# Sparse attention and a gated layer on one core: zero products into the open PSUM sums in the planner's idle stretches

## The chip, the cores and the metric

The kernel runs on one core of one Trainium2 chip. The metric is the device time of one execution in microseconds (us), the median of several runs of the same program; less is better. Engines are named as the profile names them: PE is the matrix engine (PEld its weight loads), DVE the vector engine, ACT the scalar engine, POOL the general engine, SP the engine from whose queue all DMA transfers of this kernel are issued.

## The reference

Two steps follow each other: a block-sparse attention over 4 batches of 8 heads, 768 positions and 64 columns, and a layer of 512 to 2048 to 512 columns with a rational function between its two products.

```python
scores = scale * np.matmul(q, k.transpose(0, 1, 3, 2))
mask = near blocks | first and last block | 3 sampled blocks per block of 32 rows
attn = exp(scores - max); attn = attn / (sum + 1e-09)      # masked
x = np.matmul(attn, v), heads side by side                 # 3072 x 512
h = x @ w_in
P = a[0] + a[1] * h + a[2] * h**2 + a[3] * h**3
Q = 1.0 + abs(b[0]) * abs(h) + abs(b[1]) * h**2
out = (P / (Q + 1e-06)) @ w_out                            # 3072 x 512
```

## The kernel before

The work is written down first as a list of operations (`Op`), each with an engine or a choice of engines, a price in ns, the operations that it comes after, a priority and the buffers it takes. Nothing is issued while this list is made. At the end `issue` runs through a time line of its own: at each step it takes, over all engines, the operation that can start first by its prices, writes that instruction down as the next one of its engine, and moves the engine's time forward. The order on each engine, and for the operations with a choice also the engine, come out of that time line alone. On the chip each engine then runs its row in that order, and waits by semaphores only.

The attention goes block by block (96 blocks of 32 query rows): scores (line 903, into the PSUM tile `sp`), masked maxima on DVE (913), exponentials on ACT (931), transposition (972, `pt`), its copy out of PSUM (`pT`, by `times`, line 150 on ACT), product with the values (1029, `av`). Four blocks make a half of a chunk of 256 rows, which is weighed (1063, `xn`) and transposed (1075). The layer goes in 96 units, 8 for each of 12 chunks (`unit(c, u)`): `into` (1140 to 1142, PSUM tile `ph`), the rational function on ACT and DVE (1147 to 1185, ending in `gh` and `gl`), and `out_of` (1196 to 1198), which adds the unit's products into the chunk's PSUM tile `acc`. A chunk's sum stays open from its first unit to its last. Chunk 0 is split: its first four units come first, then the eight of chunk 1, then its other four; between them a part of its sum waits in SBUF.

In the first quarter of the run the weights are also decoded from 64-bit words: loads `wl` (430, 433), three DVE steps on integers (442, 445, 448), a copy `wo_h` (`times`; ACT at line 150 or POOL at line 154), the remainder `wo_l` on POOL (459), and the like for `wi`. The keys and queries are scaled and split (`hl`, `hlq`) with the same choice of engine.

`fill` (line 157) writes a product that nobody reads. It uses the identity `ident16` as both operands and a tile `acc` of its own out of the pool of which the real sums take theirs, and starts and ends a sum with it (line 162). In `issue` the branch for PE writes such products wherever its own time line has PE waiting, as long as that time is below `fend`, 80,000 ns. Below `fend` too, it puts up to two of them ahead of an operation when its account of the current window is less than `fsh` full. That account (`tick`, `work_of`) also says whether the planner takes PE's clock to be warm; when it does not, PE's prices are multiplied by 1.8 or 2. The times of the planner's line are not those of the chip.

Of the kernel before, what the change touches and what calls it, by code (L numbers as in the profile page):

```python
# [13 lines left out]
F16 = mybir.dt.float16  # L14
# [9 lines left out]
def kernel(  # L24
# [27 lines left out]
    nc = tc.nc  # L52
    B, H, S, D = q.shape
    DM, DFF = out.shape[1], w_out.shape[0]
    P = 128
    BLK = 32
# [17 lines left out]
    const = ctx.enter_context(tc.tile_pool(name="const", bufs=1))  # L74
# [17 lines left out]
    ident16 = const.tile([P, P], F16, name="ident16")  # L92
# [60 lines left out]
        else:  # L153
            eng.tensor_scalar(out=out, in0=in_, scalar1=by, scalar2=0.0, op0=ALU.mult, op1=ALU.add)

    fills = []

    def fill():

        if not fills:  # L160
            fills.append(ps_acc.tile([P, CH // P, DM], F32, name="acc"))
        nc.tensor.matmul(fills[0][:, 0].rearrange("p (n m) -> p n m", n=DM // P), ident16, ident16.rearrange("p (o m) -> p o m", o=1).broadcast_to([P, DM // P, P]), start=True, stop=True)

    def issue(ahead):
# [11 lines left out]
        now = dict.fromkeys(todo, 500.0)  # L176
# [13 lines left out]
        fsh = 0.8  # L190
        other = {VE: 500, SC: 534.0, PO: 243.0}
        unit_of = {VE: nc.vector, SC: nc.scalar, PO: nc.gpsimd}
        slack, fend, f00, fgap = 21.0, 80000, 3000, 0
        while left:
            best = None
            for e, l in todo.items():
# [15 lines left out]
            e = o.eng  # L212
# [6 lines left out]
            if isinstance(price, list):  # L219
                for ns, size in price:  # L220
                    t = max(t, lanes.pop(0) if e == SY else t) + ns
                    dma = max(dma, t + 650) + size / 225.0
                    if e == SY:
                        lanes.append(dma + 900)
                end = dma + 900
            elif e == TE:
                f0 = max(now[e], f00)
                while f0 < fend:
                    tick(f0)
                    f = 213 if warm else 427  # L230
                    if f0 + f + fgap > t:
                        break
                    fill()
                    work_of(f0, f, 1.0)
                    f0 += f
                tick(t)
                if now[e] < fend:
                    w = window
                    x0 = w * 3413
                    for _ in range(2):  # L240
                        if not warm or t - x0 < 700 or busy.get(w, 0.0) >= fsh * (t - x0):
                            break
                        fill()
                        work_of(t, 213, 1.0)
                        t += 213
                if not warm:
                    price *= 2 if price > 1100 or price < 500 else 1.8
                work_of(t, price, o.work)
                end = t = t + price
            else:  # L250
                end = t = t + price
# [871 lines left out]
    def unit(c, u):  # L1123
# [63 lines left out]
        def out_of(e):  # L1187
            def run():
                if new and e == 0:
                    accs[c] = ps_acc.tile([P, CH // P, DM], F32, name="acc")  # L1190
                acc = accs[c]
                f = 2 * u + e
                for t in range(CH // P):
                    ghs = d["gh"][:, e * CH + t * P:e * CH + (t + 1) * P]
                    gls = d["gl"][:, e * CH + t * P:e * CH + (t + 1) * P]
                    nc.tensor.matmul(acc[:, t], ghs, wo_h[:, f], start=(new and e == 0), stop=False)  # L1196
                    nc.tensor.matmul(acc[:, t], ghs, wo_l[:, f], start=False, stop=False)  # L1197
                    nc.tensor.matmul(acc[:, t], gls, wo_h[:, f], start=False, stop=(last and e == 1))  # L1198
            return run

        def piece(lows, tiles):
# [164 lines left out]
```

## Time and profile before

| | us |
|---|---|
| median of 3 runs | 883.18 |
| lowest and highest run | 882.15, 884.92 |
| profiled execution, its own time | 884.27 |
| its span, first to last instruction | 882.5 |
| PE busy | 828.6 |
| DVE busy | 733.3 |
| ACT busy | 676.5 |
| POOL busy | 110.9 |

The last five lines belong to the one profiled execution. What lies between its time and its span is ahead of the first and behind the last instruction. An engine's busy time is the part of the span in which it ran an instruction; the time in which it stood is the rest. The granted clock is a share of full speed: 1.00 is 2.4 GHz and 0.50 is 1.2 GHz; a stretch with a value between had both. The tables by stretch are the views that show which engine is full at which time, and the chain of waits says which instruction set the time of the next.

### The profile page before, as it was taken

How to read it: one execution, taken by the hardware profiler on the slowest of the kernel's cores; microseconds unless marked ns; L12 is line 12 of the kernel's file. 1: busy time of each engine (PE TensorE's matmuls, PEld its weight loads, DVE VectorE, ACT ScalarE, POOL GpSimd, SP SyncE). 2: the span in 40 equal slices, each digit the busy share in tenths (PEclk: the TensorE clock that was granted, in tenths of full speed). 3: DMA queues.
4: the chain of work that ended last, by engine and by line, in shares of the span. 5: the costliest groups of instructions: out<-in, count | busy, mean ns of one | idle time of the engine just before them, and what ended most of it. 6: DMA issues, size and time to landing. Idle time of an engine off the chain costs nothing.

```text
span 882.5 us, 27171 instructions
## 1 busy us (share of the span) xinstructions
PE 828.6 (94%) x10339; PEld 645.5 (73%) x10339; DVE 733.3 (83%) x1749; ACT 676.5 (77%) x1447; POOL 110.9 (13%) x117
## 2 busy tenths in 40 slices
PE   8979686797899999989999999999999999999997
PEld 3545465675678787778888887777788888888886
DVE  5658998999999888778887888887878887788886
ACT  6787897897687988788867888888767688767563
POOL 1113631616310000100000000100000000000000
PEclk9999897798999999999999999999999999999999
DMA  7798689878856966799556967889556766730000
GB/s 200 178 187 197 173 181 201 221 194 228 176 150 165 287 161 159 181 214 254 168 142 160 257 179 198 199 225 259 149 144 176 200 170 156 180 106 26 1 26 24
DMA packets 240209, 151.16 MB, mean 171 GB/s; under 512 B 16208, under 2 KB 222928, under 8 KB 240080
## 3 DMA queue, kind: packets, MB, share of 16 engines
q1 hardware_dynamic: 240080, 149.43, 68.4%
q8 instruction: 82, 1.34, 0.7%
q14 instruction: 47, 0.39, 0.2%
HBM read 132.07 MB, written 11.01 MB: 162 GB/s over the span
## 4 chain that ended last, share of the span: by engine, by line
PE 70%; DVE 10%; DMA 7%; ACT 6%; SPq 4%; issue 2%; POOL 1%; ACTq 0%; DVEq 0%; POOLq 0%
PE acc L1196 9%; PE ph L1140 9%; PE acc L1198 9%; PE acc L1197 9%; PE ph L1141 8%; PE ph L1142 8%; PE av L1029 5%; PE sp L903 5%; PE pt L972 5%; DMA vg<-in_v_dram 2%; DMA wl<-in_moe_w_in_dram 2%; DMA wl<-in_moe_w_out_dram 1%; ACT kt L150 1%; PE sp L753 1%; ACT pr L931 1%
## 5 line engine op out<-in xcount | busy, mean ns | idle before, releaser
L1140 PE MATMUL ph<-xh,wi 128*128 128x256 f16 x768 | 213.5, 278 | 0.0
L1141 PE MATMUL ph<-xl,wi 128*128 128x256 f16 x768 | 212.2, 276 | 0.0
L1142 PE MATMUL ph<-xh,wi 128*128 128x256 f16 x768 | 211.9, 276 | 0.0
L1196 PE MATMUL acc<-wo_h,gh 128*128 128x512 f32 x376 | 160.4, 427 | 0.2 <-ACT ld L150 0.2
L1198 PE MATMUL acc<-wo_h,gl 128*128 128x512 f32 x376 | 150.0, 399 | 2.1 <-DVE gl L1185 2.1
L1197 PE MATMUL acc<-wo_l,gh 128*128 128x512 f32 x376 | 149.3, 397 | 0.8 <-POOL wo_l L459 0.8
L1164 DVE SCALAR_TENSOR_TENSOR ab<-sq,absb,ab 128x512 f32<-128x512 f32 x96 | 74.4, 775 | 49.9 <-ACT ab L1161 49.7
L1147 ACT ACTIVATE sq<-ph,fc 128x512 f32<-128x512 f32 x96 | 65.6, 684 | 56.9 <-PE ph L1142 56.3
L1140 PEld LDWEIGHTS <-wi 128*128 128x128 f16 x768 | 76.0, 99 | 29.2 <-issue 16.2
L913 DVE CUSTOM_DVE_ANT_1 pr<-sp,bias 128x256 f32<-128x256 f32 x224 | 84.9, 418 | 8.8 <-PE sp L903 8.4
L931 ACT ACTIVATE pr<-pr,st,cqb 128x256 f32<-128x256 f32 x112 | 66.1, 594 | 32.9 <-DVE st L942 32.9
L1175 DVE SCALAR_TENSOR_TENSOR gh<-tt,par,rr 128x512 fp32r<-128x512 f32 x96 | 72.4, 754 | 21.4 <-PE acc L1197 20.3
L1198 PEld LDWEIGHTS acc<-wo_h,gl 128*128 128x128 f32 x376 | 71.2, 189 | 19.9 <-DVE gl L1185 3.0
L1196 PEld LDWEIGHTS acc<-wo_h,gh 128*128 128x128 f32 x376 | 71.5, 190 | 17.3 <-issue 2.5
L1029 PE MATMUL av<-vg,pT 128*32 128x64 f32 x3584 | 75.6, 227 | 9.0 <-DMA vg<-in_v_dram 5.6
L1142 PEld LDWEIGHTS <-wi 128*128 128x128 f16 x768 | 76.2, 99 | 9.7
L1029 PEld LDWEIGHTS av<-vg,pT 128*32 128x32 f32 x3584 | 57.9, 113 | 33.8 <-issue 12.0
L1141 PEld LDWEIGHTS <-wi 128*128 128x128 f16 x768 | 76.2, 99 | 8.0
L972 PE MATMUL pt<-ident,pr 128*128 128x128 f32 x448 | 74.9, 289 | 7.5 <-ACT pT L150 6.8
L972 PEld LDWEIGHTS pt<-ident,pr 128*128 128x128 f32 x448 | 68.3, 205 | 18.0 <-ACT pT L150 8.0
L1197 PEld LDWEIGHTS acc<-wo_l,gh 128*128 128x128 f32 x376 | 71.4, 190 | 13.1 <-POOL wo_l L459 1.7
L150 ACT ACTIVATE pT<-pt 128x512 f32<-128x512 f32 x112 | 66.2, 591 | 14.8 <-PE pt L972 14.2
(165 smaller groups left out, 1671.6 us busy)
## 6 DMA issues: line engine op xcount, KB each, us to landing
vg<-in_v_dram SPq DMA_DIRECT2D x312, 64.0 KB, 3.4
vg<-in_v_dram SPq DMA_DIRECT2D x88, 192.0 KB, 4.0
vg<-in_v_dram SPq DMA_DIRECT2D x24, 512.0 KB, 5.7
kall<-ks SPq DMA_DIRECT2D x49, 192.0 KB, 3.6
kall<-ks SPq DMA_DIRECT2D x147, 64.0 KB, 2.0
ld<-in_k_dram SPq DMA_DIRECT2D x36, 256.0 KB, 5.0
wl<-in_moe_w_in_dram SPq DMA_DIRECT2D x32, 256.0 KB, 5.0
wl<-in_moe_w_out_dram SPq DMA_DIRECT2D x16, 512.0 KB, 4.5
```

The source lines that it names most:

```text
L150: nc.scalar.activation(out=out, in_=in_, func=AF.Copy, scale=by)
L913: nc.vector.tensor_tensor_reduce(out=prs[x][:, g].rearrange("p (s r) -> p s r", r=BLK), in0=h["sp"][:, g].rearrange("p (s r) -> p s r", r= ...
L931: nc.scalar.activation(out=prs[x][:, g], in_=prs[x][:, g], func=AF.Exp, scale=Q["first"]["c"], bias=st[:, 6 + g:7 + g], accum_out=total if ...
L972: nc.tensor.transpose(pp[:, jj * P:(jj + 1) * P], cols, ident)
L1029: nc.tensor.matmul(av[rows, g], pT[:, 2 * g + kt, rows] if plain else pT[:, 2 * g + kt, pa_, rows], vf[:, g * HG + h4, kt * D:(kt + 1) * D ...
L1140: nc.tensor.matmul(o, wh, xh[:, :, cc], start=(cc == 0), stop=False)
L1141: nc.tensor.matmul(o, wh, xl[:, :, cc], start=False, stop=False)
L1142: nc.tensor.matmul(o, wl, xh[:, :, cc], start=False, stop=(cc == NCC - 1))
L1164: nc.vector.scalar_tensor_tensor(out=d["ab"], in0=d["sq"], scalar=absb[:, 1:2], in1=d["ab"], op0=ALU.mult, op1=ALU.add)
L1196: nc.tensor.matmul(acc[:, t], ghs, wo_h[:, f], start=(new and e == 0), stop=False)
L1197: nc.tensor.matmul(acc[:, t], ghs, wo_l[:, f], start=False, stop=False)
L1198: nc.tensor.matmul(acc[:, t], gls, wo_h[:, f], start=False, stop=(last and e == 1))
```

## The change

There is a tile of zeros, `zeros16`, written once by DVE at the start. When a real sum is open, `fill` now adds a product of the identity and that tile to the sum's first half, `acc[:, 0]`, without starting or ending a sum: it adds zeros. When no real tile `acc` has been taken yet, it does as before. `summing` holds the open sums; `out_of` enters a chunk with its first product and takes it out with its last. The planner's limit `fend` goes from 80,000 to 280,000 ns, and between two sums nothing is filled in.

```diff
+    zeros16 = const.tile([P, BLK], F16, name="zeros16")
+    nc.vector.memset(zeros16, 0.0)
+    fills, summing = [], {}
...
+        if summing:
+            acc = next(iter(summing.values()))
+            nc.tensor.matmul(acc[:, 0].rearrange("p (n m) -> p n m", n=DM // BLK), ident16, zeros16.rearrange("p (o m) -> p o m", o=1).broadcast_to([P, DM // BLK, BLK]), start=False, stop=False)
+            return
...
-        slack, fend, f00, fgap = 21.0, 80000, 3000, 0
+        slack, fend, f00, fgap = 21.0, 280000, 3000, 0
...
-                while f0 < fend:
+                while f0 < fend and (summing or not accs):
...
-                if now[e] < fend:
+                if now[e] < fend and (summing or not accs):
...
+                if e == 0:
+                    summing[c] = acc
...
+                if last and e == 1:
+                    del summing[c]
```

On PE the changed program has 219 of the old products where there were 201, and 111 of the new ones. Up to its 1,422nd row PE's order is the same as before; from there the order of the real work differs too, on all engines, since the planner's time line is another. Both orders meet at the same amount of real PE work (16 units into `ph`, 13 out, 880 score products), row 3490 before and row 3749 now.

The first place is on PE, behind the second unit's products into `acc`. Before, the scores of the next block (`sp`, 903) come right behind them. Now ten zero products stand between (one is shown), and the value product and the transposition have moved ahead. Line numbers of the changed kernel are 7 to 9 higher.

```order
L972 MATMUL pt_2426<-ident_91,pr_2296 128x128 x4
L1196 MATMUL acc_2345<-wo_h_105,gh_1958 128x512
L1197 MATMUL acc_2345<-wo_l_106,gh_1958 128x512
L1198 MATMUL acc_2345<-wo_h_105,gl_2168 128x512
...
L903 LDWEIGHTS qa_2082
L903 MATMUL sp_2467<-kall_108,qa_2082 32x96
```

```order
L1205 MATMUL acc_2300<-wo_h_107,gh_2051 128x512
L1206 MATMUL acc_2300<-wo_l_108,gh_2051 128x512
L1207 MATMUL acc_2300<-wo_h_107,gl_2296 128x512
L1036 MATMUL av_115<-vg0_111,pT_2417 32x64 x16
L979 MATMUL pt_2477<-ident_91,pr_2291 128x128 x4
L165 LDWEIGHTS ident16_96
L165 MATMUL acc_2300<-zeros16_98,ident16_96 128x512
...
L910 LDWEIGHTS qa_2292
L910 MATMUL sp_2527<-kall_110,qa_2292 32x96
```

What moved: PE runs ten products more before it reaches the scores.

The second place is the last block of zero products, behind the transposition of the eighth group of queries (`hlq`). Before, the transposed probabilities and the next products into `ph` follow at once. Now 16 zero products come first, then products into `acc`, a transposition and four more zero products.

```order
L753 LDWEIGHTS hlq_4335
L753 MATMUL sp_4410<-ident16_96,hlq_4335 128x128
...
L972 MATMUL pt_4423<-ident_91,pr_4217 128x128 x4
L1140 LDWEIGHTS wi_104
L1140 MATMUL ph_4431<-xh0_114,wi_104 128x256
```

```order
L760 MATMUL sp_4539<-ident16_96,hlq_4493 128x128
...
L165 MATMUL acc_3630<-zeros16_98,ident16_96 128x512
...
L1205 MATMUL acc_3630<-wo_h_107,gh_4534 128x512
L1206 MATMUL acc_3630<-wo_l_108,gh_4534 128x512
L1207 MATMUL acc_3630<-wo_h_107,gl_4576 128x512
...
L979 MATMUL pt_4610<-ident_91,pr_4135 128x128 x4
...
L910 LDWEIGHTS qa_4561
L910 MATMUL sp_4625<-kall_110,qa_4561 32x256
```

What moved: the products into `ph` that followed the transposition are now behind twenty zero products and the next block's scores.

The third place is POOL, where the weights' remainders `wo_l` are made, at its fifth such step. Before, POOL also made the copy `wo_h` ahead of the second remainder. Now that copy is ACT's, and one of four that left POOL.

```order
L459 TENSOR_TENSOR wo_l_106<-dw_1829,wo_h_105 128x512
L154 TENSOR_SCALAR wo_h_105<-dw_1880 128x512
L459 TENSOR_TENSOR wo_l_106<-dw_1880,wo_h_105 128x512
L154 TENSOR_SCALAR hlq_1972<-ldq_1710,scq_1929 128x8x64
L154 TENSOR_SCALAR wo_h_105<-dw_1974 128x512
```

```order
L466 TENSOR_TENSOR wo_l_108<-dw_1832,wo_h_107 128x512
L466 TENSOR_TENSOR wo_l_108<-dw_1895,wo_h_107 128x512
L154 TENSOR_SCALAR hlq_2053<-ldq_1712,scq_1996 128x8x64
L154 TENSOR_SCALAR wo_h_107<-dw_2110 128x512
L466 TENSOR_TENSOR wo_l_108<-dw_2110,wo_h_107 128x512
```

What moved: up to the last weight, POOL has 5 copies `wo_h` instead of 9, 2 splits `hl` instead of 3, 2 conversions `dw` instead of 4 and 4 conversions `wi` instead of 2; the others are on ACT, which also takes the one split `hl` that DVE had.

## Rows read from the trace of the kernel before

**Rows 1.** The page: busy time of each engine, and the granted clock in the 40 slices of the span.

```profile
PE 828.6 (94%) x10339; PEld 645.5 (73%) x10339; DVE 733.3 (83%) x1749; ACT 676.5 (77%) x1447; POOL 110.9 (13%) x117
...
PEclk9999897798999999999999999999999999999999
```

**Rows 2.** Busy time by stretch: the stretch in us from the span's start, its length, busy time and instructions of each engine, the mean granted clock, the DMA share and GB/s.

```profile
0.00:60.00 60.00, 51.01 (x690) 27.97 (x690) 34.02 (x128) 43.89 (x115) 8.72 (x19) 1.00 0.83 189
0.00:95.00 95.00, 79.97 (x1053) 45.16 (x1053) 63.69 (x212) 70.00 (x175) 26.18 (x37) 0.97 0.82 185
95.00:250.00 155.00, 127.42 (x1779) 97.66 (x1775) 149.01 (x345) 128.69 (x290) 64.07 (x55) 0.89 0.84 197
250.00:882.50 632.50, 621.20 (x7512) 502.67 (x7511) 520.59 (x1194) 477.83 (x984) 20.61 (x26) 1.00 0.64 163
```

**Rows 3.** The same view for the stretches at the lower clock (their edges are rounded, so the mean is a little over 0.50): two of seven between 93.9 and 220.2 us, the sixth and the seventh; the seven are 34.1 us long together.

```profile
169.00:175.90 6.90, 4.62 (x46) 3.30 (x45) 6.90 (x9) 5.57 (x13) 3.92 (x3) 0.53 0.74 203
213.40:220.20 6.80, 6.24 (x41) 4.54 (x42) 6.80 (x19) 4.93 (x16) 3.57 (x3) 0.52 0.90 256
```

**Rows 4.** Who DVE waited for between 95 and 250 us: total us, times, longest.

```profile
DVE xn L1063 <- PE av L1029: 1.5, 1, 1.5
```

**Rows 5.** The chain of waits between 95 and 250 us, in order of time (start us, us, engine, tile and line): of its 195 longest pieces the first and the last of 47 on ACT (31.8 us together), and of 26 on PE (10.8 us together) the first, two at the full clock and three of the last seven.

```profile
94.51 1.26 ACT pr L931 x4
...
109.58 0.60 PE sp L753 x8
...
119.84 0.24 PE acc L1196
...
121.02 0.23 PE acc L1198
...
171.08 1.01 PE sp L678 x8
172.09 0.53 PE acc L1196
...
174.33 0.44 PE acc L1198
...
202.83 0.59 ACT pr L931 x2
```

**Rows 6.** The same chain between 213.4 and 220.2 us, shares by engine, tile and line.

```profile
by line: DVE ab L1178 18.7%; DVE ab L1164 14.6%; DVE gl L1185 9.7%; DVE tt L1157 9.7%; DVE tt L1181 9.7%; DVE gh L1175 9.6%; DVE tt L1154 8.9%; DVE dw L445 8.8%; DVE sc L348 3.0%; DVE scq L348 2.9%; issue 2.5%; DVE sm L953 2.3%; DVE st L942
```

**Rows 7.** DVE and POOL side by side: one row of each engine's instructions in order of time (start us, us), then groups of DVE instructions by form (busy us, mean ns of one), first between 95 and 250 us, then between 400 and 700 us, where POOL hardly runs.

```profile
169.49 1.75 DVE L445 SCALAR_TENSOR_TENSOR wi<-wl,wi 128x512 int32<-128x512 int32 x1
...
169.31 1.38 POOL L459 TENSOR_TENSOR wo_l<-dw,wo_h 128x512 fp32r<-128x512 f32 x1 [1.29 <-ACT wo_h L150]
...
L1164 DVE SCALAR_TENSOR_TENSOR ab<-sq,absb,ab 128x512 f32<-128x512 f32 x11 | 10.2, 926 | 1.3 <-ACT ab L1161 1.3
L942 DVE TENSOR_SCALAR st<-st,cq 128x2 f32<-128x2 f32 x16 | 7.3, 462 | 0.1
...
L1164 DVE SCALAR_TENSOR_TENSOR ab<-sq,absb,ab 128x512 f32<-128x512 f32 x39 | 29.4, 753 | 21.0 <-ACT ab L1161 20.9
L942 DVE TENSOR_SCALAR st<-st,cqb 128x2 f32<-128x2 f32 x35 | 7.8, 222 | 0.0
```

**Rows 8.** Groups by form between 95 and 250 us, of the copies and splits that change engine: on POOL, on ACT, on DVE (busy us, mean ns of one).

```profile
L154 POOL TENSOR_SCALAR wo_h<-dw 128x512 fp32r<-128x512 f32 x9 | 7.9, 876 | 32.7 <-DVE dw L448 30.1 <-DVE mx L613 2.0 <-DVE scq L351 0.6
...
L154 POOL TENSOR_SCALAR hl<-ld,sc 128x512 f16<-128x512 f32 x3 | 3.5, 1153 | 7.4 <-PE sp L678 3.9 <-DMA vg<-in_v_dram 3.6
...
L150 ACT ACTIVATE wo_h<-dw 128x512 fp32r<-128x512 f32 x6 | 3.8, 630 | 2.3 <-DVE dw L448 2.3
L150 ACT ACTIVATE hl<-ld,sc 128x512 f16<-128x512 f32 x2 | 1.4, 761 | 0.0
...
L154 DVE TENSOR_SCALAR hl<-ld,sc 128x512 f16<-128x512 f32 x1 | 0.5, 480 | 0.0
```

**Rows 9.** PE's instructions in order of time (start us, us; in brackets the idle time before, and what ended it): two rows of the old fills, then the places at which the new ones come in.

```profile
86.92 0.60 PE L162 MATMUL acc<-ident 128*128 128x512 f16 x2
...
87.83 1.89 PE L162 MATMUL acc<-ident 128*128 128x512 f16 x8
...
127.12 0.23 PE L903 MATMUL sp<-kall,qa 128*32 128x96 f16 x4
...
129.59 0.65 PE L1029 MATMUL av<-vg,pT 128*32 128x64 f32 x32 [1.58 <-DMA vg<-in_v_dram]
...
141.40 0.27 PE L903 MATMUL sp<-kall,qa 128*32 128x96 f16 x4 [0.96 <-DVE sc L348]
...
144.08 1.08 PE L1029 MATMUL av<-vg,pT 128*32 128x64 f32 x32 [1.64 <-DMA vg<-in_v_dram]
...
175.93 0.50 PE L1196 MATMUL acc<-wo_h,gh 128*128 128x512 f32 x1 [0.24 <-ACT ld L150]
...
184.55 1.09 PE L972 MATMUL pt<-ident,pr 128*128 128x128 f32 x4 [0.41 <-ACT pr L931]
...
242.07 0.65 PE L1029 MATMUL av<-vg,pT 128*32 128x64 f32 x32 [0.78 <-ACT pT L150]
...
250.51 0.50 PE L1197 MATMUL acc<-wo_l,gh 128*128 128x512 f32 x1 [0.36 <-POOL wo_l L459]
```

More of the change, by code (lines that the diff above doesn't have):

```diff
@@ L154, in times @@
             eng.tensor_scalar(out=out, in0=in_, scalar1=by, scalar2=0.0, op0=ALU.mult, op1=ALU.add)
-    fills = []
+    zeros16 = const.tile([P, BLK], F16, name="zeros16")
+    nc.vector.memset(zeros16, 0.0)
+    fills, summing = [], {}
     def fill():
+        if summing:
+            acc = next(iter(summing.values()))
+            nc.tensor.matmul(acc[:, 0].rearrange("p (n m) -> p n m", n=DM // BLK), ident16, zeros16.rearrange("p (o m) -> p o m", o=1).broadcast_to([P, DM // BLK, BLK]), start=False, stop=False)
+            return
         if not fills:
```

## The prediction

> **What bounds the kernel now.** I read first the busy times and the slices of the clock [rows 1]. PE is busy 828.6 of 882.5 us, and the clock leaves full speed almost only in the first third. So I cut the run in stretches [rows 2]. From 250 us to the end PE is busy 621.20 of 632.50 us at a granted clock of 1.00: there PE is the bound, and the change touches little of that stretch. Up to 95 us PE's order is the same before and after (the first 1,422 rows), so nothing is to be had there either. The change works between 95 and 250 us, and there the picture is another: PE is busy 127.42 of 155 us, so it stands 27.6 us, and its granted clock is 0.89 on average; DVE is busy 149.01 of the 155. The lower clock comes in seven stretches, 34.1 us together, of which two are shown [rows 3]. At half speed 34.1 us do the work of 17 us at full speed. That is the largest number the change could claim: 17 us of PE's time. But a full engine beside it sets the pace. In both of the stretches of rows 3 DVE is busy from end to end (6.90 of 6.90, 6.80 of 6.80), and DVE waited for PE once in the 155 us, for 1.5 us [rows 4]. So what PE's time is worth must be read from the chain of waits.
>
> **The clock.** In the chain between 95 and 250 us, PE has 26 of the longest pieces, 10.8 us of 155, or 7% [rows 5]. In the stretch from 213.4 to 220.2 us the chain names DVE alone [rows 6]; only in the one from 169 us has it PE, from 171.08 to 174.77 us: eight small transpositions in 1.01 us and six products into `acc` in 2.68 us. At the full clock the like took 0.60 us and 0.24 us each [rows 5], together 2.04 us. If the new products hold the clock there, the chain is shorter by 3.69 - 2.04 = **1.6 us**. The bounds are 0 (DVE, full at the same time, takes the chain over) and 6.0 us, all that DVE stands between 95 and 250 us [rows 2]. I take 1.6, the piece that the chain shows.
>
> **The new products.** One of the old fills takes (1.89 - 0.60) / 6 = 0.215 us in a row at the full clock [rows 9]. There are 129 more (18 old, 111 new): 27.7 us, as much as PE stands there. They are free where PE waits anyhow. I laid the blocks beside the waits of the same place before [rows 9]. The 18 old ones and 50 of the new stand ahead of waits at least as long as they. The others do not: ten ahead of scores that before ran at 127.12 us with no wait (2.15 us); 16 around the waits of 0.96 and 1.64 us at 141.40 and 144.08 (3.44 - 2.60 = 0.84 us over); 13 where PE waited 0.24 and 0.41 us at 175.93 and 184.55 (2.15 us over); and 22 at the end, where it waited 0.78 and 0.36 us at 242.07 and 250.51 (4.73 - 1.14 = 3.59 us over). That is 8.7 us of PE's time in front of work that was ready. For the first three I take PE's share of the chain, 7% of 5.1 = 0.4 us. The last block stands close to the point at which PE becomes the bound, so more of it counts: I take a quarter, 0.9 us, since DVE is still full up to there. Together **+1.3 us**, between 0 and 8.7.
>
> **Work that changes engine.** POOL loses four copies `wo_h` and one split `hl` (4 x 0.876 + 1.153 = 4.7 us [rows 8]); the two conversions `dw` that leave it and the two `wi` that come to it are of one shape and cancel. ACT gets four `wo_h` and two `hl`, 4 x 0.630 + 2 x 0.761 = 4.0 us. It has 26.3 us of idle time for them [rows 2], but ACT is also 31.8 of the chain's 155 us [rows 5]; I take that share, a fifth: **+0.8 us**, between 0 and 4.0. DVE gives one `hl` away: **-0.5 us** [rows 8], which counts in full, since DVE is full; at the least nothing. And DVE's instructions are longer while POOL runs: the two forms shown take 926 and 462 ns here against 753 and 222 ns where POOL hardly runs [rows 7]. That is 11 x 0.173 + 16 x 0.240 = 5.7 us beside 64.07 us of POOL, 0.09 us for each; 4.7 us less of POOL give back **-0.4 us**. The least is 0, the most 4.7, if DVE stood for the whole of each. The row that looks like that is the product on integers that began at 169.49 us and took 1.75 us, beside a POOL instruction from 169.31 on [rows 7]; I take the lower value, since most of POOL's time shows no such row. The Trainium skill (SBUF — State Buffer, section Who interferes with whom) has it that DVE and POOL share one pair of ports, and that who holds it holds it for a whole instruction while the other stands. By that rule up to the whole 4.7 us come back and the sum would be -4.7; the trace agrees in the long row, and not in the average.
>
> The tile of zeros is one small write ahead of everything and costs nothing that can be seen. The order on SP's queue changes too, with the same number of transfers; which load is earlier where I cannot price, and it is in the range only.
>
> **The sum.** -1.6 + 1.3 + 0.8 - 0.5 - 0.4 = -0.4 us. The profiled execution took 884.27 us (span 882.5 us and 1.8 us around it), so 883.9; it lies 1.1 us over the median of 883.18, so the forecast for the median is **882.8 us**: nothing that can be told from no change. A measurement of this kernel tells about 0.3%, 2.6 us: faster is below 880.5, slower above 885.8.
>
> **Rival 1, DVE gets free.** POOL's 4.7 us come back whole, and the last block of zero products costs nothing because DVE is the bound to the end of the stretch: -1.6 + 0.4 + 0.8 - 0.5 - 4.7 = -5.6 us, 877.6. For it: DVE is busy 149.01 of 155 us, so each of its us counts, and the long row at 169.49. Against it: the average of the forms shown, and that ACT, which takes the work over, is itself a fifth of the chain. The far end of this side is that DVE's 6.0 us of idle time all go and 0.9 us of its work: 876.3.
>
> **Rival 2, the zero products are in the way.** PE runs its row in order. If DVE and ACT keep the pace they had, the ready work behind the four blocks starts 8.7 us later in all, and PE, which is the bound from 250 us on, never gets that back: +8.7 - 1.6 + 0.8 - 0.5 - 0.4 = +7.0 us, 890.2. The place is the last block above all, 22 products at about 244 us. It decides from the point at which half of the 8.7 us lies on the path: 1.7 us only cancel the three gains less ACT's 0.8, and from 1.7 + 2.6 = 4.3 us the kernel is measurably slower. For it: PE waits only 1.14 us around that place. Against it: DVE is fuller than PE up to 250 us, and work delayed on PE there mostly waits for DVE anyhow.
>
> **Rival 3, zeros do not hold the clock.** Then the clock between 95 and 250 us stays near 0.89, the 1.6 us are not gained, and the products take 0.43 us each. The 39 of the first three blocks cost 16.8 - 3.3 = 13.5 us, 7% of it 0.9; the 22 of the last 9.5 - 1.1 = 8.3, a quarter of it 2.1: +3.0 + 0.8 - 0.5 - 0.4 = +2.9 us, 886.1. Against it: up to 60 us the old fills multiply an identity with itself, nearly all zeros, and the granted clock is 1.00 there with PE busy 51.01 of 60 us [rows 2].
>
> **How the numbers follow.** The forecast has 0.45, of which 0.10 falls below 880.5 and 0.02 above 885.8. Rival 1 has 0.27, all of it faster; rival 2 has 0.23, all slower; rival 3 has 0.05, 0.03 of it slower. That gives faster 0.37, same 0.35, slower 0.28. The range goes from the far end of rival 1 to that of rival 2, 876.0 to 890.5, and leaves out about 0.15. The forecast's own range is 880 to 886.
>
> **What the profile after would show.** If the steps are right: a granted clock of 0.97 or more between 95 and 250 us; PE busier there by some 20 us with no more idle time than 10 us or so; DVE still busy over 145 of 155 us; POOL's busy time less by about 5 us and ACT's more by about 4; and the point at which PE becomes the bound, the last remainder `wo_l` on POOL (250 us now), within 2 us of where it is. Rival 1 would show DVE's forms near their undisturbed times and that point some 5 us earlier; rival 2 shows it late, with the scores and products behind the zero blocks starting late and DVE standing behind PE; rival 3 a clock near 0.89. The forecast is wrong if the stretch from 250 us on changes by itself: its order is nearly the same and its 11.3 us of idle time are few, but they are waits that hang on where loads land.

## The result, and the profile after

| kernel | runs | median, us | lowest to highest | ratio to before, 95% interval |
|---|---|---|---|---|
| before | 6 | 883.53 | 878.91 to 884.92 | 1 |
| after | 6 | 889.69 | 888.74 to 893.93 | 1.0072 [1.0046, 1.0098] |

The changed kernel is slower by 0.7%. Its median lies 6.9 us above the forecast of 882.8 us and just inside the far end of the range, 890.5 us. The profiled execution has a span of 887.7 us (before 882.5). The page of after, busy times and granted clock [rows 1 for before]:

```profile
PE 845.2 (95%) x10468; PEld 650.6 (73%) x10468; DVE 727.9 (82%) x1749; ACT 681.0 (77%) x1455; POOL 107.2 (12%) x110
...
PEclk9999999999999999999999999999999999999999
```

Busy time by stretch, columns as in [rows 2]:

```profile
95.00:250.00 155.00, 138.27 (x1870) 98.44 (x1863) 141.03 (x344) 128.75 (x290) 59.26 (x49) 0.99 0.85 197
250.00:887.70 637.70, 624.66 (x7570) 505.96 (x7568) 523.71 (x1197) 482.46 (x993) 21.73 (x24) 1.00 0.64 162
```

The change did what its words say: the clock between 95 and 250 us went from 0.89 to 0.99, and PE is busy 10.9 us more there. But DVE, the full engine of that stretch, is busy 8.0 us less (141.03 for 149.01): it stands 14.0 of the 155 us where it stood 6.0. Where it stands is in the view of what DVE waited for between 95 and 260 us (total us, times, longest):

```profile
DVE wi L449 <- POOL wi L154: 6.9, 4, 4.2
...
DVE scq L355 <- PE sp L350: 1.9, 1, 1.9
```

The second wait is not in the same view of before. The first has a shorter counterpart there, at which ACT makes the conversion (L442 is L449 of the changed kernel):

```profile
DVE wi L442 <- ACT wi L150: 1.7, 2, 1.6
```

The longest wait in the changed kernel, in order of time on DVE (start us, us; in brackets the idle time before):

```profile
145.33 0.23 DVE L949 TENSOR_SCALAR st<-st,cq 128x2 f32<-128x2 f32 x1
149.74 0.43 DVE L449 TENSOR_SCALAR wi<-wi 128x512 int32<-128x512 int32 x1 [4.18 <-POOL wi L154]
```

The chain of waits says what POOL itself waited for, a load of packed weights that was issued at 141.80 us:

```profile
141.80 7.11 DMA wl<-in_moe_w_in_dram
...
149.05 0.66 POOL wi L154
```

The load is hardly later than before, though. There the same conversion also starts as soon as its load has landed, on ACT at 148.23 us:

```profile
148.23 0.67 ACT L150 ACTIVATE wi<-wl 128x512 f32<-128x512 f32 x1 [1.16 <-DMA wl<-in_moe_w_in_dram]
```

What differs is what DVE has to do until then. Before, 13 more of its instructions stand ahead of that step, two splits `hl` among them; in the changed kernel they stand behind it:

```profile
144.25 0.48 DVE L154 TENSOR_SCALAR hl<-ld,sc 128x512 f16<-128x512 f32 x1
144.76 1.64 DVE L386 SCALAR_TENSOR_TENSOR hl<-ld,sc,hl 128x512 f16<-128x512 f32 x2
...
148.93 0.43 DVE L442 TENSOR_SCALAR wi<-wi 128x512 int32<-128x512 int32 x1 [1.57 <-ACT wi L150]
```

On PE of the changed kernel, in order of time, zero products are followed by a wait, and the scale of the key (L350, on `mx`) stands behind 48 products of `into`, from 145.04 us on:

```profile
141.54 1.89 PE L165 MATMUL acc<-zeros,ident 128*128 128x512 f16 x8
144.60 0.61 PE L760 MATMUL sp<-ident,hlq 128*128 128x128 f16 x8 [1.16 <-DVE xl L1094]
145.04 0.27 PE L1147 MATMUL ph<-xh,wi 128*128 128x256 f16 x1
...
150.28 0.27 PE L350 MATMUL sp<-ident,mx 128*128 128x128 f32 x1
```

Before, that scale ran at 140.14 us. So the trace offers two readings. **Theory A**, the prediction's second rival: the zero products stand in front of ready work on PE. **Theory B**: the products are harmless, and what costs is that the planner, which now counts them on its time line, deals out all the *real* work of all engines in another order. The experiments first tell these apart, then look for the piece of the order that costs. All were timed in five rounds beside the kernel before; each ratio is to its runs on the same chip, whose median was 882.68 us for the first four kernels and 882.13, 882.79, 884.16 and 882.72 us for the later groups.

### The profile page after: what moved, and what is told of

It is laid out like the page before. It is cut to its first block, busy times and chain, and to the rows that moved or that the text cites. A ratio compares the mean times of both kernels' runs of the same rounds, so it can differ in the third digit from the quotient of the medians.

```text
span 887.7 us, 27434 instructions
## 1 busy us (share of the span) xinstructions
PE 845.2 (95%) x10468; PEld 650.6 (73%) x10468; DVE 727.9 (82%) x1749; ACT 681.0 (77%) x1455; POOL 107.2 (12%) x110
## 4 chain that ended last, share of the span: by engine, by line
PE 60%; DVE 11%; DMA 9%; ACT 8%; SPq 7%; issue 4%; POOL 0%; ACTq 0%; POOLq 0%; DVEq 0%
PE acc L1205 8%; PE ph L1147 7%; PE acc L1207 7%; PE acc L1206 7%; PE ph L1149 6%; PE ph L1148 6%; PE av L1036 5%; PE pt L979 4%; PE sp L910 4%; DMA vg<-in_v_dram 3%; DMA ldq<-in_q_dram 2%; SPq L1006 2%; ACT pr L938 2%; PE acc L169 2%; DMA wl<-in_moe_w_in_dram 1%
## 5 line engine op out<-in xcount | busy, mean ns | idle before, releaser
L1147 PE MATMUL ph<-xh,wi 128*128 128x256 f16 x768 | 211.0, 275 | 3.0 <-DVE tt L1164 2.9
L1149 PE MATMUL ph<-xh,wi 128*128 128x256 f16 x768 | 209.9, 273 | 0.0
L1148 PE MATMUL ph<-xl,wi 128*128 128x256 f16 x768 | 209.9, 273 | 0.0
L1171 DVE SCALAR_TENSOR_TENSOR ab<-sq,absb,ab 128x512 f32<-128x512 f32 x96 | 72.2, 752 | 49.5 <-ACT ab L1168 49.4
L1147 PEld LDWEIGHTS <-wi 128*128 128x128 f16 x768 | 75.3, 98 | 28.0 <-issue 15.6
L1036 PE MATMUL av<-vg,pT 128*32 128x64 f32 x3584 | 73.8, 223 | 11.6 <-DMA vg<-in_v_dram 5.9
L1182 DVE SCALAR_TENSOR_TENSOR gh<-tt,par,rr 128x512 fp32r<-128x512 f32 x96 | 74.5, 776 | 12.2 <-PE acc L1206 11.9
L1148 PEld LDWEIGHTS <-wi 128*128 128x128 f16 x768 | 75.4, 98 | 10.5 <-issue 3.0
L1149 PEld LDWEIGHTS <-wi 128*128 128x128 f16 x768 | 75.4, 98 | 8.9
L938 ACT ACTIVATE pr<-pr,st,cq 128x256 f32<-128x256 f32 x112 | 65.9, 592 | 12.5 <-DVE st L949 12.4
L979 PEld LDWEIGHTS pt<-ident,pr 128*128 128x128 f32 x448 | 67.3, 204 | 10.5 <-ACT pr L938 2.0
```

Of the source, the lines that this page charges most:

```text
L938: nc.scalar.activation(out=prs[x][:, g], in_=prs[x][:, g], func=AF.Exp, scale=Q["first"]["c"], bias=st[:, 6 + g:7 + g], accum_out=total if ...
L979: nc.tensor.transpose(pp[:, jj * P:(jj + 1) * P], cols, ident)
L1036: nc.tensor.matmul(av[rows, g], pT[:, 2 * g + kt, rows] if plain else pT[:, 2 * g + kt, pa_, rows], vf[:, g * HG + h4, kt * D:(kt + 1) * D ...
L1147: nc.tensor.matmul(o, wh, xh[:, :, cc], start=(cc == 0), stop=False)
L1148: nc.tensor.matmul(o, wh, xl[:, :, cc], start=False, stop=False)
L1149: nc.tensor.matmul(o, wl, xh[:, :, cc], start=False, stop=(cc == NCC - 1))
```

## Products or order?

**The order alone**: the planner counts as in the changed kernel, but no product of zeros is issued.

```diff
         if summing:
-            acc = next(iter(summing.values()))
-            nc.tensor.matmul(acc[:, 0]..., zeros16..., start=False, stop=False)
             return
```

> The changed kernel without its 111 zero products; the planner still counts them, so every engine's row of real work is that of the changed kernel. Theory A (the products stand in front of ready work, 8.7 us of PE's time): the time falls back to that of before, 882 to 885 us. Theory B (the new order of the real work costs, the products are nearly free): it stays slow, 888 to 892 us, with a granted clock below 0.93 between 95 and 250 us.

**The products alone**: the planner counts as before, and the real work has the old order. In the idle time that the planner sees anyway, zero products are issued without being counted (64 of them, and 13 more of the old kind).

```diff
+        slack, fend, f00, fgap = 21.0, 80000, 3000, 0
+        zend = 280000
...
+                if f0 >= fend and t < zend and (summing or not accs):
+                    for _ in range(int((t - f0) / 213)):
+                        fill()
```

> The kernel before, every row of real work in its old order, with 64 zero products and 13 more of the old ones where the old time line has PE idle after 80,000 ns. Theory A: 77 x 0.215 = 16.6 us of products, about half of it in front of ready work, so 886 to 889 us. Theory B: within 2 us of before, and 1 to 2 us below it if the clock rises as forecast; the granted clock between 95 and 250 us above 0.95.

**The products alone, denser** (`/ 123` in place of `/ 213`; 120 of zeros, 24 more old ones).

> The same with 120 zero products and 24 more of the old ones, 1.7 for each that would fit by the old time line. Theory A: worse than the kernel with 77, by 5 us or more, 890 us or over. Theory B: PE has 27.6 us of idle time and 17 us of clock to give, so still within 3 us of before.

**Up to the first sum**: the changed kernel with only the old kind of product, as long as no sum has been opened.

```diff
-                while f0 < fend and (summing or not accs):
+                while f0 < fend and not accs:
...
-                if now[e] < fend and (summing or not accs):
+                if now[e] < fend and not accs:
```

> The changed kernel with products only until the first sum is opened: 219 old ones, none with zeros; the planner counts none after that. Both theories: within 2 us of before if the cost arises while sums are open. If it is 887 us or more, the cost comes from the 18 old products or from the order that they alone bring.

| kernel | median, us | ratio, 95% interval |
|---|---|---|
| order alone | 894.34 | 1.0137 [1.0108, 1.0165] |
| products alone | 879.64 | 0.9971 [0.9950, 0.9993] |
| products alone, denser | 881.31 | 0.9985 [0.9964, 1.0006] |
| up to the first sum | 893.71 | 1.0136 [1.0110, 1.0163] |

Theory A falls. Without any zero product the new order is slower still; with 120 of them in the old order nothing is lost. The gain of the products is 882.68 - 879.64 = 3.0 us on the old order (with the denser ones 1.4 us, which is not clear of nothing) and 894.34 - 889.69 = 4.7 us on the new one (5.7 us by the ratios, 0.65%). The new order costs 894.34 - 882.68 = 11.7 us without zero products, and 889.69 - 879.64 = 10.1 us with products on both sides. The last kernel missed its expectation, which was within 2 us of before by either theory: it costs as much as the order alone. Its 18 more products of the old kind are not the cause as such, since the kernel with the new order up to 137 us, below, has them too and is not slower than before.

The stretch from 95 to 250 us, first of the order alone:

```profile
95.00:250.00 155.00, 123.96 (x1736) 94.24 (x1735) 139.94 (x339) 126.95 (x286) 59.67 (x49) 0.89 0.83 197
```

and then of the products alone:

```profile
95.00:250.00 155.00, 135.13 (x1860) 100.44 (x1861) 148.38 (x347) 129.46 (x294) 64.04 (x55) 0.97 0.84 199
```

The clock goes with the products (0.89 without, 0.97 with), DVE's standing with the order (15.1 us in the new one, 6.6 in the old). Where do the products gain? In the window from 205 to 229 us, around the half-clock stretch of [rows 6], first before, then the products alone:

```profile
205.00:229.00 24.00, 20.03 (x246) 15.32 (x245) 22.30 (x51) 17.06 (x37) 10.38 (x9) 0.86 0.81 199
```

```profile
205.00:229.00 24.00, 21.84 (x283) 16.50 (x282) 24.00 (x52) 18.89 (x41) 10.82 (x10) 1.00 0.84 199
```

DVE no longer stands there. Its one wait for PE, the 1.5 us of [rows 4], lay in this window and is gone. The real order is the same in both kernels, so the same instruction can be compared: `gl` starts at 229.0 us before and at 226.6 us with the products alone, and the 2.4 us stay.

That is half of the 4.8 us between these two profiled executions. The other large piece comes far behind the last zero product (233.9 us): the `gl` at 377.2 us before is 2.3 us earlier, the one at 397.6 us is 4.3 us earlier. Between them PE waits for the transposed keys (`kt`) in both, before for 2.5 us and then with a half-clock stretch, with the products alone for 1.7 us and at the full clock. The wait, first before, then the products alone:

```profile
PE sp L903 <- ACT kt L150: 2.5, 1, 2.5
```

```profile
PE sp L914 <- ACT kt L150: 1.7, 1, 1.7
```

and the window from 380 to 390 us in the same order:

```profile
380.00:390.00 10.00, 7.52 (x102) 6.12 (x101) 6.31 (x18) 8.02 (x18) 0.00 (x0) 0.83 1.03 235
```

```profile
380.00:390.00 10.00, 9.15 (x160) 7.44 (x160) 7.01 (x20) 9.56 (x23) 0.00 (x0) 1.00 0.94 239
```

The new order shows the like: without zero products the clock is 0.83 from 360 to 370 us and from 485 to 495 us, behind waits of PE of 2.1 and 3.0 us; in the changed kernel these waits are 1.0 and 1.3 us and the clock is 1.00. So part of the gain arises behind 250 us, at waits of PE that came out shorter. No run separates that part or shows why.

## Which piece of the order?

For the next kernels the planner's result was written out as a table (operation, engine, products ahead of it) and issued from there; the order is then the same as the planned one, row for row, on all engines, until the table is edited. Four tables splice the old order with its products (879.6) and the new one with its products (889.7):

```diff
-            best = None
-            for e, l in todo.items():
-                ...
+            n, x, k = rows.pop(0)
+            o, e = plan[n], (VE, SC, PO, TE, SY, None)[x]
```

> The order of the work is written out as a table instead of being planned: up to about 137 us it is the old order (that of the kernel before, with the new products in its waits as in the run of the products alone), after that the rest in the new order with the new products. All engines and queues are cut at the same place of the plan. Nothing is left out. The two ends are known: 879.6 us all old, 889.7 us all new. Theory MIDDLE (the new order loses its time between 137 and 195 us, where the key's scale stands behind 48 products on the matrix engine and DVE stands behind a conversion of the weights): 887 to 891. Theory EARLY (what is loaded and done up to 137 us already lags): 878 to 882. Theory LATE (the loss is in the order from 195 us on): 887 to 891. Theory NO PLACE (any plan of that kind scatters by 1 per cent, and a mixture is a third plan): anywhere, up to 895.

> The counterpart: the new order with its products up to about 137 us, then the rest in the old order with the products in its waits. Nothing is left out. MIDDLE: 878 to 882. EARLY: 887 to 891. LATE: 878 to 882. NO PLACE: not bound to add up with the run before to 879.6 + 889.7.

> As the first, but cut at about 195 us: old order up to there, new order behind it. Nothing is left out. MIDDLE and EARLY: 878 to 882. LATE: 887 to 891. NO PLACE: anywhere.

> The counterpart: new order up to about 195 us, old order behind it. Nothing is left out. MIDDLE and EARLY: 887 to 891. LATE: 878 to 882. NO PLACE: anywhere, and with the run before it not bound to add up.

| new order | median, us | ratio, 95% interval |
|---|---|---|
| nowhere (products alone) | 879.64 | 0.9971 [0.9950, 0.9993] |
| up to 137 us | 881.69 | 0.9997 [0.9973, 1.0021] |
| up to 195 us | 887.69 | 1.0053 [1.0031, 1.0076] |
| from 195 us | 886.91 | 1.0052 [1.0031, 1.0073] |
| from 137 us | 892.25 | 1.0106 [1.0071, 1.0141] |
| everywhere (after) | 889.69 | 1.0072 [1.0046, 1.0098] |

The piece from 137 to 195 us costs 0.56% behind the new order (1.0053 - 0.9997) and 0.54% behind the old one (1.0106 - 1.0052): some 5 us both times. That piece is found, and DVE stands in it: of the 58 us from 137 to 195 us it is idle for 9.7 and 9.3 us in the kernels that have the new order there, and for 4.2 and 2.4 us in those that have the old one. In this order: new up to 195 us, from 137 us, up to 137 us, from 195 us:

```profile
137.00:195.00 58.00, 46.91 (x555) 33.58 (x556) 48.26 (x114) 47.98 (x105) 19.70 (x18) 0.94 0.89 202
137.00:195.00 58.00, 46.32 (x626) 33.92 (x627) 48.67 (x113) 46.66 (x102) 19.74 (x18) 0.94 0.85 195
137.00:195.00 58.00, 47.67 (x626) 34.48 (x624) 53.84 (x116) 49.93 (x112) 19.43 (x17) 0.91 0.89 210
137.00:195.00 58.00, 48.08 (x700) 35.92 (x700) 55.62 (x130) 52.21 (x117) 18.82 (x17) 0.97 0.93 215
```

It doesn't stand for one thing, however. DVE's longest wait there, new up to 195 us and then new from 137 us:

```profile
DVE wi L429 <- POOL wi L154: 6.9, 3, 5.0
```

```profile
DVE xl L1074 <- ACT xh L150: 3.0, 2, 2.9
```

The rest doesn't add up: the order from 195 us on costs 0.8% behind the old order, where theory MIDDLE expected no cost, and 0.2% behind the new one, which is within the intervals. What it costs behind the old one is partly a wait far from every zero product. What PE waited for between 440 and 500 us in the kernel with the new order from 195 us:

```profile
PE av L1016 <- ACT pT L150: 3.5, 1, 3.5
```

Before, PE waited for nothing in that window; in the changed kernel the same wait is 1.3 us.

Two edits of the table of after test what stands out between 137 and 195 us. **The key's scale first**: 15 operations (`mx`, its steps, the splits `hl`, their transpositions and evacuations) 23 places earlier, ahead of the 48 products. **POOL's conversions**: three of them on ACT again. The table itself is packed in the kernel; the lines say what was done to it.

```diff
+ch = [743, 744, 745, 746, 747, 749, 755, 750, 756, 751, 752, 757, 753, 758, 759]
+rows = moved(rows, ch, earlier_by=23)
```

> The new order with its products, written out as a table; one thing is moved: the scale of the key tile (the transposition of mx on the matrix engine, its steps on DVE), the two splits hl, their transpositions and evacuations stand 23 places of the plan earlier, ahead of the four halves of into (48 products), at about the place that they had in the old order. Nothing is left out; unchanged it takes 889.7 us. Theory SCALE (the middle stretch loses its 5 to 6 us because the key's scale stands behind the 48 products): 884 to 886. Theory DVE BEHIND WI (it loses them because DVE's row stands 6.9 us behind the weights' conversion): no change, 888 to 891. Theory MANY PLACES: a gain of at most 2 us, 887.5 to 890.

```diff
-[199, POOL] [217, POOL] [242, POOL]
+[199, ACT] [217, ACT] [242, ACT]
```

> The new order with its products, written out as a table; three conversions of the packed weights that the new plan gave to POOL (one dw, two wi) are on ACT again, as in the old plan, at the same place of the order. Nothing is left out; unchanged it takes 889.7 us. Theory POOL (DVE waits 6.9 us for POOL's wi because POOL is slow and late): 883 to 887. Theory LOAD (POOL is only named: the conversion itself waits for the load of wl, which lands at 149 us in either case): 888 to 891, and the wait stays, now named after ACT.

The scale first took 890.21 us, 1.0098 [1.0070, 1.0125]; POOL's conversions on ACT 890.04 us, 1.0092 [1.0061, 1.0124]. Neither gives anything back. In the second DVE's long wait is still there, under another name, in order of time on DVE and then on ACT:

```profile
145.96 0.23 DVE L929 TENSOR_SCALAR st<-st,cq 128x2 f32<-128x2 f32 x1
149.50 0.43 DVE L429 TENSOR_SCALAR wi<-wi 128x512 int32<-128x512 int32 x1 [3.32 <-ACT wi L150]
```

```profile
148.80 0.67 ACT L150 ACTIVATE wi<-wl 128x512 f32<-128x512 f32 x1 [0.50 <-DMA wl<-in_moe_w_in_dram]
```

The conversion waits for the load whichever engine has it, and DVE, which runs its row in order, has nothing else ahead of the next step. The engine named in a wait was only the last link. With the scale first DVE waits as well, 3.6 us for the same conversion, and for other things besides:

```profile
DVE wi L429 <- POOL wi L154: 5.7, 3, 3.6
...
DVE hl L373 <- ACT hl L150: 1.6, 2, 1.1
DVE pr L900 <- PE sp L890: 1.5, 2, 1.1
```

So neither the scale's place alone nor POOL is what costs. No run took DVE's wait behind the load away by itself, and which exchange in this piece costs the five us is not shown.

## A rule, or one deal of many?

When zero products are laid in without being counted the order is the old one, so the new order comes from the count alone. The count acts in two ways: the planner takes PE to be at full clock and no longer doubles its prices, and its second rule puts up to two products ahead of an operation that is ready. And there is a third possibility: the list of work is dealt out greedily, and any small cause deals it anew. Two nudges of the kernel *before*, without a zero product:

```diff
-    MARGIN = 17.0
+    MARGIN = 18.0
```

> The kernel before with one constant of the planner nudged: MARGIN 18 ns in place of 17 (what it adds to each hand-over between engines). No product is added, nothing is left out. The order differs from the old one from the same place on as that of the change (row 1,404 of the matrix engine). Theory LOTTERY (the old plan is a good one among many, and anything that deals the order anew from about 95 us on costs about as much as the change's order alone, 894.3, whatever was counted): 888 to 897. Theory COUNTED (the new order is worse because the planner counts the products as work that is in the way): 880 to 886.

```diff
-    HELD = 0.5
+    HELD = 0.52
```

> The kernel before with another constant of the planner nudged: HELD 0.52 in place of 0.5 (the share by which DVE is reckoned slower beside POOL). No product is added, nothing is left out; the order differs from the old one from row 244 of DVE on. LOTTERY: 888 to 897. COUNTED: 880 to 886.

Then the price alone, in both directions, in the kernel before, and the first rule alone in the changed one:

```diff
-                if not warm:
+                if not warm and now[e] < 80000:
```

> The kernel before, whose planner never doubles the price of an operation of the matrix engine from 80 us on: it takes that engine to be at full clock, as the products make the changed planner do. No product is added, nothing is left out; the order is a new one. Theory PRICE (a planner that believes the full clock deals a worse order): 888 to 897. Theory SECOND RULE or DEAL: within 0 to 0.5 per cent above the kernel before, 882 to 888.

```diff
-                if not warm:
+                if not warm or 80000 <= now[e] < 250000:
```

> The kernel before, whose planner doubles every price of the matrix engine between 80 and 250 us, as if its clock were half there throughout. No product is added, nothing is left out; the order is a new one. PRICE, if the planner gains by reckoning low: 876 to 884; DEAL: 882 to 890; a price that is wrong by so much more than the real clock of 0.89 may also cost by itself: up to 895.

```diff
-                if now[e] < fend and (summing or not accs):
+                if now[e] < 80000:
```

> The changed kernel, with its second rule (up to two products ahead of an operation that is ready, which the plan puts later by 213 ns each) ended at 80 us as before; the first rule, which fills waits, goes on to 280 us: 214 old products and 103 of zeros. Nothing is left out. PRICE: 886 to 892. SECOND RULE: 877 to 883. DEAL: anywhere from 878 to 892.

And three more deals of the changed planner (a deal is one order that the planner comes out with): `MARGIN` 18, `HELD` 0.52, and POOL's surcharge 250 in place of 243.

> The changed kernel with the constant MARGIN at 18 ns in place of 17, which in the kernel before made no difference (882.8): another deal of the changed planner, with 218 old products and 87 of zeros. Nothing is left out. PRICE or SECOND RULE: 886 to 893, as the changed kernel. DEAL (the change had an unlucky one): 878 to 886.

> The changed kernel with HELD at 0.52 in place of 0.5: another deal of the changed planner, with 221 old products and 79 of zeros. Nothing is left out. Its counterpart without the change took 886.6. UNLUCKY DEAL (the products gain about 0.3 to 0.5 per cent on any order, and the change's own order was a bad one): 879 to 886. RULE (the changed planner deals badly, and 879.6 was luck): 887 to 895.

> The changed kernel with the planner's surcharge for work given to POOL at 250 ns in place of 243: a third deal of the changed planner, with 221 old products and 104 of zeros. Nothing is left out. UNLUCKY DEAL: 877 to 886. RULE: 887 to 895.

The table has all of it, with the us that DVE stands between 95 and 250 us (155 less its busy time in the profiled run).

| kernel | median, us | ratio, 95% interval | DVE stands, us |
|---|---|---|---|
| changed, MARGIN 18 | 879.55 | 0.9952 [0.9931, 0.9973] | 6.8 |
| products alone | 879.64 | 0.9971 [0.9950, 0.9993] | 6.6 |
| changed, first rule only | 881.55 | 0.9976 [0.9958, 0.9995] | 5.6 |
| products alone, denser | 881.31 | 0.9985 [0.9964, 1.0006] | 6.4 |
| before, price full | 882.72 | 0.9993 [0.9977, 1.0010] | 9.2 |
| new order up to 137 us | 881.69 | 0.9997 [0.9973, 1.0021] | 7.5 |
| before, MARGIN 18 | 882.81 | 0.9999 [0.9981, 1.0017] | 10.5 |
| before | 882.68 | 1 | 6.0 |
| before, HELD 0.52 | 886.62 | 1.0051 [1.0033, 1.0070] | 10.4 |
| changed, HELD 0.52 | 886.61 | 1.0052 [1.0033, 1.0071] | 15.8 |
| changed, POOL 250 | 887.53 | 1.0052 [1.0032, 1.0073] | 13.7 |
| new order from 195 us | 886.91 | 1.0052 [1.0031, 1.0073] | 6.6 |
| new order up to 195 us | 887.69 | 1.0053 [1.0031, 1.0076] | 11.9 |
| after | 889.69 | 1.0072 [1.0046, 1.0098] | 14.0 |
| after, POOL's conversions on ACT | 890.04 | 1.0092 [1.0061, 1.0124] | 14.5 |
| after, scale first | 890.21 | 1.0098 [1.0070, 1.0125] | 16.6 |
| new order from 137 us | 892.25 | 1.0106 [1.0071, 1.0141] | 12.8 |
| up to the first sum | 893.71 | 1.0136 [1.0110, 1.0163] | 17.6 |
| order alone | 894.34 | 1.0137 [1.0108, 1.0165] | 15.1 |
| before, price half | 920.97 | 1.0411 [1.0390, 1.0433] | 19.2 |

That a planner reckons with the full clock is not enough to make it slower: without a zero product it stays at 882.72 us. (Reckoning with half of it throughout costs 4%, more than was expected of it.) That is one deal, so it doesn't clear the price altogether. With the second rule ended at 80 us the changed kernel takes 881.55 us, without the loss; but the second rule isn't needed as a cause: 1 ns more in `MARGIN` leaves both rules in force and takes the changed kernel from 889.7 to 879.55, which beats the kernel before and has the lowest median found (its interval overlaps that of the products alone). Its stretch from 95 to 250 us, and what DVE waited for there:

```profile
95.00:250.00 155.00, 140.63 (x1909) 102.38 (x1898) 148.16 (x351) 131.87 (x297) 63.55 (x53) 0.98 0.87 199
```

```profile
DVE xn L1070 <- PE av L1036: 2.3, 3, 1.1
DVE wi L449 <- ACT wi L150: 1.9, 3, 1.2
```

PE is as busy as in after and the clock is held as well; the 6.9 us behind the conversion are not there. So the change has two parts that can be had one without the other: products that gain, and a deal of the order that cost more than they gain. Apart from the spliced kernel whose loss lies behind 250 us, every kernel that is slower beyond its interval has DVE standing 10.4 us or more between 95 and 250 us, and every one that isn't has 10.5 or less. That is a link and not yet a cause: the two groups touch, and DVE's standing comes from one execution of each kernel (that of before with `MARGIN` 18 was the slowest of its twelve).

## Why the prediction was wrong, by its own steps

**The step that failed** is the one that the prediction passed over: "The order on SP's queue changes too ...; which load is earlier where I cannot price, and it is in the range only." The order of the real work got no term in the sum, apart from the copies that change engine. It is the largest term: +11.7 us measured without zero products, 10.1 us with them. About five of these belong to the order between 137 and 195 us, where DVE stands 9.3 to 9.7 us of 58 in place of 2.4 to 4.2. Which exchange there costs them is not shown, and the rest was not pinned to one place. It was not a later load, either: the load that DVE stands behind longest lands within a us of where it did, and DVE has less ahead of it.

**DVE stays full** was the second half of the same mistake. The prediction let DVE's 149.01 of 155 us hide what happens on PE, and named "DVE still busy over 145" as its sign. It came at 141.03. An engine is full as long as its row has something ready, and that is a property of the order that the change deals anew.

**The clock** came as said (0.99, sign 0.97 or more), and rival 3 falls: zeros hold it. The size, 1.6 us, is near what 205 to 229 us gave back (DVE 1.7 us busier), but that is luck, since the place was wrong. The prediction took the stretch from 169 us, because the chain names PE there, and gave the one from 213 us nothing, because the chain names DVE alone [rows 6]. Measured, the first gave half a us at most: `gl` starts at 171.2 us in before and in the products alone, and further on at 184.5 and 184.0. Behind the second it is 2.4 us earlier. The half-clock stretch at 384 us, on PE's own path, got no term. DVE's only wait for PE [rows 4] was the row to go by.

**The new products** and the clock together were forecast at +1.3 - 1.6 = -0.3 us. Measured together they are -3.0 us with 77 products and -1.4 with 144 on the old order, and -4.7 with the change's own 111 of zeros on the new one: a larger gain than forecast. No run gives the products' own part beside the clock's, so whether +1.3 has the wrong sign stays open. PE is busier by 10.9 us and not by 20, and stands 16.7 and not under 10, since the clock's gain comes off its busy time and the new order adds waits. Rival 2, which expected 8.7 us of delay, comes near the measured time and is wrong in its mechanism: with no zero product in the way the kernel is 4.7 us slower, not faster. That the measured time lies within the range at all is owed to this rival's price.

**Work that changes engine** (+0.8 for ACT, -0.5 for DVE, -0.4 for POOL) was not measured by itself: the one run on it gave three other conversions (one `dw`, two `wi`) back to ACT and changed nothing. POOL's busy time in the stretch fell by 4.8 us as forecast; ACT's rose by 4.5 over the whole run (681.0 for 676.5), but stayed at 128.75 (128.69) in the stretch, where 4 more were expected. Rival 1 lived on POOL's time coming back to DVE. DVE's busy time over the whole run is indeed 5.4 us less (727.9 for 733.3), but the time that this frees was stood, and in the kernel with the new order up to 195 us, whose POOL is as busy as before (110.8 us), it is 728.7 as well. By the rule of the Trainium skill that the prediction weighed (SBUF — State Buffer, section Who interferes with whom) up to all of POOL's 4.7 us would have come back; with DVE no longer full, these runs can't show whether the rule holds.

**The last remainder** `wo_l` on POOL was to stay within 2 us of where it was (248.9 us). It came at 253.2, 4.3 us late. That was named as a sign of rival 2, and it came without that rival's mechanism. The warning that the forecast fails "if the stretch from 250 us on changes by itself" came true in part: the order from 195 us on costs 0.2 to 0.8%, depending on what stands ahead of it.

**What stays open.** Four deals of the changed planner took 879.6, 886.6, 887.5 and 889.7 us, four of the old one (the price alone among them) 882.7, 882.7, 882.8 and 886.6. Of the three nudges of the changed planner one took what an unlucky deal had led to expect, one what a rule had, and one (886.6) lies between. That doesn't settle whether counting the products makes for worse deals on the whole, or whether the change's own was an unlucky one. Why planning with only the old products up to the first sum comes out as badly as the order alone wasn't tried further, nor was the order of SP's queue alone: loads and engines share buffers, so one order can't be taken without the other.

## What to carry to other kernels

Where a greedy planner sets the order, an edit to what it counts is two changes, the edit and a new deal of everything behind it. Price the deal too, as a scatter: here 880 to 890 us for the changed planner and 883 to 887 for the old one, where the edit itself is worth 3 to 6 us. To measure the edit, hold the order fixed (issue the new work uncounted, or replay the order from a table); to use it, deal several times and keep the best. And where one engine is full, read a diff of orders for what that engine used to do while a load was on its way, and not only for the engine that the change is about.

## What the runs showed of the hardware

Products with an operand of zeros hold PE's clock: with 111 of them, 0.38 us each from start to end and 0.22 us apart in a row of eight, which takes 1.89 us, the granted clock between 95 and 250 us is 0.99, where the same order without them has 0.89.

A held clock was worth much less than its half-clock time suggests: before, 34.1 us lay at half clock between 93.9 and 220.2 us, and on the same order the products gave back 3.0 us. In the profiled executions half of the gain came on DVE, the full engine, behind its one wait for PE; the stretch of 6.9 us at 169 us gave half a us at most, with DVE busy through all of it; and some 2 us came around 384 us, at a wait of PE, which is the bound there.
